# A strided and local attention with a gated MLP on one core: another kernel's planner numbers for batches 0 to 2, the planner's engine rule fixed later on, one ring for each x tile, new keys for batches 3 to 7

## The chip, the cores and the metric

One NeuronCore of a Trainium2 chip runs the kernel. The time is the device time of one launch in microseconds (us). Of the kernel before there are three timed runs; one more execution was profiled, and every time of a single instruction is from that one. PE is TensorE (matmul), PEld its weight loads, DVE VectorE, ACT ScalarE, POOL GpSimd, SP SyncE, which issues all DMAs of this kernel.

## The reference, cut to what matters

```python
# q, k, v: (8, 8, 576, 64): batch, heads, sequence, head size; everything in fp32
scores = q @ k.T / 8
mask_local   = (rel >= 0) & (rel < 32)                  # heads 0 to 3, rel = row - column
mask_strided = (rel >= 0) & (column % 32 == row % 32)   # heads 4 to 7
attn = softmax(where(mask, scores, -1e9))
x = heads side by side of (attn @ v)                    # (8, 576, 512)
h = relu(x @ w_in)                                      # w_in: 512 x 1024
u, v = h[..., :512], h[..., 512:]
v_n = (v - mean(v)) / sqrt(var(v) + 1e-6)               # over the last axis
v_s = einsum('ts,bsd->btd', w_spatial, v_n) + b_spatial[None, :, None]   # 576 x 576
out = (u * v_s) @ w_out                                 # w_out: 512 x 512
```

## The kernel before, in words

**Work.** The kernel goes through eight batches. A batch has four **x tiles** (t = 4 x batch + hp), each of 128 rows (two heads) by 576 columns; hp 0 and 1 are pairs of local heads (`local_attention`), hp 2 and 3 of strided heads (`strided_attention`). For each: scores on PE (L565 local, L711 strided), the softmax on DVE and ACT (in the first batches with a mask that DVE applies while it takes the maximum, L602), a transpose on DVE (L646, L765), copies into a sparse block layout (`ptl`, `pts`; ACT or POOL), the product with v (L675 and L781, called the PV product), and the copy of the result into x (`evac_x`).

fp32 operands of large products are held as two numbers, a high part (`rnd`, L427 on ACT, L429 on DVE or POOL) and a low part (`rest`, L437, a subtraction with two SBUF operands or one in PSUM); a product takes three matmuls (high x high, high x low, low x high). So every weight and every activation is split before PE can use it. The weights come in as 64-bit words and are first turned into fp32 by a few steps on ACT, POOL and DVE (L866, L875, L883), w_out is also combined into seven blocks (L902), and `spatial_weights` splits the spatial weights into `wsp_sb`.

Per batch follow: **V** (`v_tile`, L1034: four blocks of 128 rows, one of the 64 rows left over, the "tail", which from batch 2 on is made for two batches at once); the chain of the normalisation (`chain`: relu on ACT L992, statistics on DVE L997 and L1001 and L1005, a power on POOL L1010, the scaling on DVE L1017), a split of the result into `vn`; **U** (L1234 in batches 0 to 2; in batches 3 to 7 a Strassen form, `moe_u`, L1157); the **spatial** product (L1331, the tail's part L1343 and L1344), the gate (L1354, L1356); the **output product** in a Strassen form (L1435, its additions L1463) and the store (L1456).

**What sets the order.** All instructions go through `Program.add(key, choices, fn, reads, writes, ...)`. `Program.order()` then walks over a model of the engines: whenever an engine is free it takes the ready operation with the lowest key, and for an operation with several choices it picks the engine on which it would end first by the model's costs. The order so found is written out as it is; each engine runs its instructions in that order, and waits for what they need. DMAs (`load`) are in that order too, all on SyncE. The keys come from the table `KEYS`: "a" for the attention tiles of batches 0 and 1, "lq" and "lw" for their loads, "v", "u", "s", "t", "o" for the weights and "lv", "lu", "ls", "lo" for their loads, "fill" and "set" for clearing buffers, "p", "b" and "p2", "b2" for the steps of the output product, "cl", "ta", "la", "su", "tu" for the later batches. "dp" is a handicap that DVE gets in the choice between DVE and POOL (one number for operations with two SBUF operands that lock the port, one for the others), until "dpt" (in thousands of ns of the model's time); `SLOWED` is the model's slowdown when DVE and POOL work side by side. "w" sets where PE gets idle matmuls on zeros (L1622) to hold its clock.

**Buffers.** `r_x` holds two rings of four x tiles, one for batch 1 and its like, one for the others. The second is also the place into which the spatial weights are loaded before they are split (`spatial_weights`), and later a place for weights (`raw_slots`). `kbd` holds the strided keys, two halves that are filled and read in turn; `xt` (`r_xt`) holds the values of a strided tile or the tail rows, and `w_out_sb`, while no weights are in it, the q and v of the first strided tiles (`early_q`, `early_v`).

## Time and profile before

| | |
|---|---|
| median of 3 runs | 517.21 us (516.7 to 517.56) |
| profiled execution | 518.85 us |
| its span, from first to last instruction | 517.0 us |
| PE busy | 494.2 us (96%) |
| DVE busy | 407.8 us (79%) |
| ACT busy | 270.9 us (52%) |
| POOL busy | 142.3 us (28%) |
| mean granted clock of PE | 0.979 |
| DMA | 52.65 MB, 102 GB/s over the span |

The profiled execution is 1.85 us longer than its span (what lies around the instructions) and 1.64 us above the median of the timed runs. A line of a timeline is start, duration, engine, line, operation, output <- inputs, shape, how many were merged, and in brackets how long the engine waited for what. A line of a group has the number of instructions, their busy time, the mean of one in ns and the idle time ahead of them. In a chain or a timeline "PE L1331" is line 1331 of the kernel.

### The profile page before, as it was taken

Reading aid. Unit: us, or ns where it says so; the run is one execution under the profiler, and the core shown is the slowest. Engines: PE = TensorE matmul, PEld = TensorE weight load, DVE = VectorE, ACT = ScalarE, POOL = GpSimd, SP = SyncE. Lnnn points to the kernel's source line nnn. Section 1 sums busy time; section 2 is a strip of 40 time slices with the busy share of each in tenths; the row PEclk is TensorE's granted clock in tenths of the full one; section 3 lists DMA queues with packets and bytes.
Section 4 is the critical chain, followed back from the end, with each engine's and each line's share of the span. In section 5 each row is a group of like instructions: output and inputs, shape, how many; then the busy total and the mean of one; then the engine's idle time right before and its main releaser. Section 6 shows DMA issues by size and latency. Waiting matters only on the chain.

```text
span 517.0 us, 14639 instructions
## 1 busy us (share of the span) xinstructions
PE 494.2 (96%) x5824; PEld 451.1 (87%) x5824; DVE 407.8 (79%) x1140; ACT 270.9 (52%) x801; POOL 142.3 (28%) x256
## 2 busy tenths in 40 slices
PE   6779979999999999899999999999999998999997
PEld 4558879989899899899899998999899997899897
DVE  2799899969489769998699958997699648784566
ACT  5786765569453685476354646457264414241222
POOL 3455864043222134211131306212120102210200
PEclk9688989999999999999999999999999999999999
DMA  8796522444035413233033603324030300011002
GB/s 273 296 335 231 182 83 81 168 123 135 2 125 159 144 49 115 93 112 109 2 119 113 195 2 94 115 67 129 1 97 20 115 1 2 1 46 47 1 1 93
DMA packets 26244, 52.65 MB, mean 102 GB/s; under 512 B 3136, under 2 KB 11584, under 8 KB 26176
## 3 DMA queue, kind: packets, MB, share of 16 engines
q1 hardware_dynamic: 26176, 51.72, 30.1%
q8 instruction: 46, 0.75, 0.6%
q14 instruction: 22, 0.18, 0.1%
HBM read 42.27 MB, written 9.44 MB: 100 GB/s over the span
## 4 chain that ended last, share of the span: by engine, by line
PE 79%; DVE 10%; DMA 4%; POOL 2%; ACT 2%; issue 1%; SPq 1%; POOLq 0%; DVEq 0%; ACTq 0%
PE m L1034 17%; PE m L1331 17%; PE m L1435 15%; PE m L1157 10%; PE m L1234 5%; PE po L781 4%; PE po L675 3%; PE s L565 2%; PE m L1343 2%; DMA outT<-vv 2%; PE s L711 1%; DVE x L437 1%; DVE vn L437 1%; PE m L1344 1%; DMA k<-kT 1%
## 5 line engine op out<-in xcount | busy, mean ns | idle before, releaser
L1331 PE MATMUL m<-wsp_sb,vn 128*128 128x288 f32 x720 | 106.4, 299 | 5.3 <-DVE wsp_sb L437 3.8
L1331 PEld LDWEIGHTS m<-wsp_sb,vn 128*128 128x128 f32 x720 | 100.1, 191 | 7.4 <-DVE wsp_sb L437 4.1
L1034 PE MATMUL m<-w_in_sb,x 128*128 128x512 f32 (+1 forms) x408 | 100.9, 403 | 0.0
L1034 PEld LDWEIGHTS m<-w_in_sb,x 128*128 128x128 f32 (+1 forms) x408 | 75.5, 188 | 19.4 <-DVE x L437 0.2
L992 ACT ACTIVATE vv<-m 128x512 f32<-128x512 f32 (+1 forms) x37 | 21.8, 596 | 65.8 <-PE m L1034 65.3
L429 POOL TENSOR_SCALAR ptl<-pc 32x320 f32<-32x320 f32 (+3 forms) x86 | 41.5, 483 | 53.1 <-PE po L675 18.8
L1435 PE MATMUL m<-g,w_out_sb 128*128 128x288 f32 x384 | 55.5, 296 | 0.0
L622 ACT ACTIVATE pl<-pl,ml 128x64 f32<-128x64 f32 (+1 forms) x140 | 47.2, 341 | 15.3 <-DVE ml L602 15.1
L1010 POOL TENSOR_TENSOR bn<-bn,sel 128x1 f32<-128x1 f32 (+1 forms) x37 | 21.8, 593 | 115.1 <-DVE bn L1005 114.1
L1435 PEld LDWEIGHTS m<-g,w_out_sb 128*128 128x128 f32 x384 | 52.4, 188 | 0.3 <-DVE o L1463 0.2
L1435 PE MATMUL m<-vn,w_out_sb 128*128 128x288 f32 x288 | 42.1, 297 | 0.0
L997 DVE BATCH_NORM_STATS2 bn<-vv 128x6 f32<-128x512 f32 (+1 forms) x37 | 25.4, 686 | 19.8 <-ACT vv L992 19.5
L429 POOL TENSOR_SCALAR pts<-pc 32x288 f32<-32x288 f32 x37 | 17.5, 472 | 84.8 <-DVE pc L765 59.1
L1234 PE MATMUL m<-x,w_in_sb 128*128 128x288 f32 x288 | 40.2, 297 | 0.0
L1435 PEld LDWEIGHTS m<-vn,w_out_sb 128*128 128x128 f32 x288 | 39.2, 188 | 0.7 <-DVE o L1463 0.2
L427 ACT COPY ptl<-pc 32x64 f32<-32x64 f32 (+3 forms) x106 | 36.4, 345 | 6.0 <-DVE pc L646 3.1
L1234 PEld LDWEIGHTS m<-x,w_in_sb 128*128 128x128 f32 x288 | 38.8, 188 | 0.7
L1017 DVE TENSOR_SCALAR vv<-vv,bn 128x512 f32<-128x512 f32 (+1 forms) x37 | 21.2, 572 | 13.9 <-POOL bn L1010 13.7
L427 ACT CAST g<-u 128x576 fp32r<-128x576 f32 (+1 forms) x33 | 20.0, 610 | 19.2 <-DVE u L1356 12.7
L1168 DVE TENSOR_TENSOR u<-m,vv 128x288 f32<-128x288 f32 x30 | 13.4, 449 | 18.7 <-PE m L1157 18.6
L622 ACT ACTIVATION_READ_ACCUMULATOR pl<-pl,ml 128x1 f32 (+1 forms) x140 | 26.8, 191 | 0.0
L437 DVE TENSOR_TENSOR g<-u,g 128x576 fp32r<-128x576 f32 (+1 forms) x40 | 24.5, 631 | 0.8 <-ACT g L427 0.7
(187 smaller groups left out, 967.1 us busy)
## 6 DMA issues: line engine op xcount, KB each, us to landing
q<-qT SPq DMA_DIRECT2D x30, 295.0 KB, 4.2
outT<-o SPq DMA_DIRECT2D x48, 144.0 KB, 1.8
k<-kT SPq DMA_DIRECT2D x16, 304.0 KB, 4.3
kbd<-ks SPq DMA_DIRECT2D x32, 144.0 KB, 3.6
v_raw<-vl SPq DMA_DIRECT2D x11, 384.0 KB, 5.0
v_raw<-vs SPq DMA_DIRECT2D x8, 512.0 KB, 5.1
xt<-vs SPq DMA_DIRECT2D x7, 512.0 KB, 3.6
outT<-vv SPq DMA_DIRECT2D x16, 144.0 KB, 1.8
```

What stands on the lines that cost most here:

```text
L427: eng.copy(dst(), src())
L429: eng.tensor_scalar(dst(), src(), 1.0, 0.0, op0=ALU.mult, op1=ALU.add)
L437: eng.tensor_tensor(dst(), src(), f32(hi()), op=ALU.subtract)
L622: eng.activation(p_sb()[:m, u, :], src, AF.Exp, bias=st()[:m, u : u + 1], scale=SCALE if masked else -1.0, **total,)
L992: lambda eng: eng.activation(v()[:m], v_ps()[:m, :], AF.Relu), [(v_ps,)], [(v,)],
L997: lambda eng: eng.bn_stats(bn()[:m, 0:6], v()[:m]), [(v,)], [(bn,)],
L1010: lambda eng: eng.tensor_tensor(bn()[:m, 9:10], bn()[:m, 8:9], sel[:m, 0:1], op=ALU.pow),
L1034: eng.matmul(v_ps()[:m, :], x_at(kt)[:, a, :], w_in_sb[:, w, kt, HF:], start=(n == 0 and i == 0), stop=(n == NT - 1 and i == 2),)
L1157: eng.matmul(o_ps()[:, :HS], w_at(w)[:, a * P : (a + 1) * P], x_at(j), start=first and kk == 0 and i == 0, stop=kk == 1 and i == 2, skip_g ...
L1234: eng.matmul(u_ps()[:, :HS], w_in_sb[:, w, kt, f * P : (f + 1) * P], xs[NHP * b + kt]()[:, a, r], start=(n == 0 and i == 0), stop=(n == NT ...
L1331: eng.matmul(s_ps()[:, :HS], vn()[:, a, kt, fs], wsp_sb[:, w, kt, r], start=(kt == 0 and i == 0), stop=False,)
L1435: eng.matmul(o_ps()[:, :HS], w_out_sb()[:, b_at, w, kk, a * P : (a + 1) * P], at(j, kk), start=first and kk == 0 and i == 0, stop=kk == 1 ...
```

## The change

The functions `next_x`, `pv` and `weight` are new, and so is the field `turn` of a buffer.

* **Planner's numbers.** All keys of `KEYS` are replaced. Those that bear on batches 0 to 2 are another kernel's, those for batches 3 to 7 are new. So are the model's costs of POOL: 125 for 200 in `rnd`, 170 for 245 in its blocked form, 150 for 190 in `lowest`, the slowdowns in `SLOWED`, and a weight of 2 for POOL there (`weight`). The normalisation's scaling is counted as a light user of the port (`share=2`).
* **Engine rule.** The handicap "dp" now holds only to 125 us of the model's time; from there on it is `HELD`, the pair of numbers that was in force before all along.
* **Rings.** `r_x` is now eight rings of one tile. `next_x` gives them out: 0, 1, 2, 3 to 7 for batches 0 and 1 and the spatial weights in the order in which they ask, then 0, 1, 2; later tiles take 3 + t mod 4. Since a ring of one has no order among its tiles, `turn` makes a tile wait for the first use of the one handed out before it, in the early batches. `raw_slots` takes rings 7, 0, 1, 2.
* **PV key.** From batch 3 on the PV product's key is moved by "pv" (9.73 later-batch local tiles, 0.08 strided, -202.13 from tile 28 on; it is subtracted).

```diff
-    "a": (-7906.0, -7964.0, -15830.5, -4267.6, 1379.5, 702.2, 2039.1, -3334.8,),
+    "a": (-8700.2, -14417.0, -7800.0, -6389.1, 679.9, 5260.8, 7132.0, -3152.0,),
...
-    "dp": (12894.8, -1038.4,),
-    "dpt": (657.16,),
+    "dp": (6774.7, -492.7,),
+    "dpt": (125.0,),
...
+    "pv": (9.73, 0.08, -202.13,),
...
+HELD = (12894.8, -1038.4)
...
-SLOWED = ((0.3, 0.15), (0.45, 0.6), (0.9, 0.8))
+SLOWED = ((0.2, 0.3), (0.33, 1.2), (1.2, 0.5))
...
-                if buf.n >= buf.ring.bufs:
+                if buf.n > buf.ring.bufs:
                     deps.update(buf.last.users[:1])
+                if buf.turn is not None:
+                    deps.update(buf.turn.users[:1])
...
+        def weight(n, e):
+            return 2 if e == POOL and self.share[n] else self.share[n]
...
-                    slow = SLOWED[max(share, self.share[n])]
+                    slow = SLOWED[max(share, weight(n, e))]
...
-            held = KEYS["dp"][locks] if now < KEYS["dpt"][0] * 1000.0 else 0.0
+            held = (KEYS["dp"] if now < KEYS["dpt"][0] * 1000.0 else HELD)[locks]
...
-    r_x = [Ring(sb, f"x{i}", [P, 2, S], F32R, NHP) for i in range(2)]
+    r_x = [Ring(sb, f"x{i}", [P, 2, S], F32R, 1) for i in range(2 * NHP)]
+    x_made, x_next = [], iter([0, 1, 2, *range(3, 8), 0, 1, 2])
...
-        cost = {ACT: 110 + 0.87 * n, DVE: 70 + 0.52 * n, POOL: 200 + (1.65 if apart else 1.0) * n}
+        cost = {ACT: 110 + 0.87 * n, DVE: 70 + 0.52 * n, POOL: 125 + (1.65 if apart else 1.0) * n}
...
-        x_homes = [r_x[1].new() for _ in range(NHP)]
+        x_homes = [r_x[i].new() for i in (7, 0, 1, 2)]
...
-                due - 1.5, [(PE, 6 * 98)], f_v, [*vin, *ptok], [(o_ps,)],
+                due - 1.5 - pv(t), [(PE, 6 * 98)], f_v, [*vin, *ptok], [(o_ps,)],
...
+    def next_x(t=None):
+        at = next(x_next) if t is None or t < LEAD * NHP else 3 + t % NHP
+        buf = r_x[at].new()
+        if len(x_made) > 8 and (t is None or t < ALONE):
+            buf.turn = x_made[-1]
+        x_made.append(buf)
+        return buf
+
+    def pv(t):
+        return KEYS["pv"][2 if t >= 28 else t % NHP // 2] if t >= ALONE else 0.0
...
-        xs[t] = r_x[b == 1].new()
+        xs[t] = next_x(t)
...
-                buf = r_x[1].new()
+                buf = next_x()
```

In the changed kernel the lines behind the table are shifted: L565 is L573, L602 is L610, L437 is L445, L457 is L465, L1034 is L1057 and L1331 is L1354. The order has 1434 rows on PE (1419 before), 1125 on DVE (1131), 523 on ACT (512), 219 on POOL (207) and 182 on SyncE (184).

On SyncE, the first loads of the program; `w_out_sb <- qT` and `kbd <- ks` are the q and k of a strided tile, `q_0` and `k_0` those of a local tile, `xt <- vs` and `v_raw` are values, `vn <- w_in` is a weight. Before:

```order
L457 DMA w_out_sb_84<-qT 128x590
L457 DMA xt_87<-vs 128x1024
L457 DMA cst_sb<-cst 128x192
L457 DMA o_98<-eye 128x128
L457 DMA vn_101<-w_in 128x1024
L457 DMA kbd<-ks 64x576 x2
L457 DMA q_0_123<-qT 128x590
L457 DMA k_0_134<-kT 128x608
L457 DMA v_raw_0_140<-vl 128x768
```

and now:

```order
L465 DMA cst_sb<-cst 128x192
L465 DMA vn_85<-w_in 128x1024
L465 DMA o_92<-eye 128x128
L465 DMA q_0_94<-qT 128x590
L465 DMA k_0_100<-kT 128x608
L465 DMA q_0_107<-qT 128x590
L465 DMA k_0_121<-kT 128x608
L465 DMA v_raw_0_135<-vl 128x768
L465 DMA xt_177<-vs 128x1024
```

The q and k of a local tile moved ahead of everything of the strided ones, and both local tiles come first.

Also on SyncE, the later loads of batch 0, where the `kbd` rows for the second strided tile's successor wait until the scores before them have read the buffer. Before:

```order
L457 DMA w_out_sb_84<-qT 128x590
L457 DMA kbd<-ks 64x576 x2
L457 DMA w_out_sb_84<-vs 128x1024
L457 DMA q_1_336<-qT 128x590
L457 DMA g_378<-w_in 128x1024
L457 DMA kbd<-ks 64x576 x2
L457 DMA vn_101<-w_in 128x1024
L457 DMA g_377<-w_in 128x1024
```

and now:

```order
L465 DMA w_out_sb_228<-qT 128x590
L465 DMA kbd<-ks 64x576 x2
L465 DMA w_out_sb_228<-vs 128x1024
L465 DMA g_347<-w_in 128x1024
L465 DMA q_1_390<-qT 128x590
L465 DMA kbd<-ks 64x576 x2
L465 DMA u_291<-w_in 128x1024
L465 DMA q_1_432<-qT 128x590
L465 DMA v_raw_1_477<-vs 128x1024
L465 DMA kbd<-ks 64x576 x2
```

Behind the `kbd` rows that overwrite the buffer there stand loads of w_in, before and now, and now one more pair of q and v loads.

On DVE, the end of the stretch between the last x tile of batch 0 and the first spatial product; `pl_75 <- s` (with a second instruction that writes `ml_77`) is a masked maximum of a local tile of batch 1, `vv` and `vn` belong to the normalisation of batch 0, `g` to w_out, `wsp_sb` to the spatial weights. Before, with rows between them that are alike:

```order
L437 TENSOR_TENSOR vn_767<-vv_841,vn_767 128x512
L437 TENSOR_TENSOR w_out_sb_822<-g_648,w_out_sb_822 128x256
L602 ISA pl_75,ml_77<-s_777,cst_sb 128x64
L602 ISA ml_77 128x1
L602 ISA pl_75,ml_77<-s_779,cst_sb 128x64
L602 ISA ml_77 128x1
...
L437 TENSOR_TENSOR w_out_sb_822<-g_735,w_out_sb_822 128x256 x2
L437 TENSOR_TENSOR wsp_sb<-x_0_604,wsp_sb 128x576 x2
```

and now:

```order
L445 TENSOR_TENSOR w_out_sb_895<-g_638,w_out_sb_895 128x256 x2
L445 TENSOR_TENSOR vn_742<-vv_837,vn_742 128x512
L445 TENSOR_TENSOR wsp_sb<-x_0_714,wsp_sb 128x576
L1005 TENSOR_TENSOR wt_b<-x_0_843,wt_b 96x576
L610 ISA pl_76,ml_78<-s_744,cst_sb 128x64
L610 ISA ml_78 128x1
```

The maxima of the next local tile, which stood ahead of the last split of the spatial weights, now stand behind it, and so does a part of w_out.

64 lines of the change are left out of this document (34 added, 30 removed), and 8 rows, old and new, of the table KEYS.

## The prediction

> **What bounds the kernel now.** First the busy times of the page, then the same by stage (the stretches are mine: two halves of the head, then the batches), then the chain of waits, then the timelines of PE and DVE in the head. The page:
>
> ```profile
> PE 494.2 (96%) x5824; PEld 451.1 (87%) x5824; DVE 407.8 (79%) x1140; ACT 270.9 (52%) x801; POOL 142.3 (28%) x256
> ```
>
> By stretch (length, then PE, PEld, DVE, ACT, POOL busy, granted clock, share of the DMA engines, GB/s):
>
> ```profile
> 0.00:35.00 35.00, 24.82 (x472) 16.33 (x472) 21.25 (x48) 24.31 (x63) 15.69 (x35) 0.85 0.84 292
> 35.00:70.00 35.00, 30.84 (x351) 26.93 (x352) 32.28 (x97) 25.77 (x83) 24.52 (x30) 0.89 0.64 222
> 70.00:205.00 135.00, 135.00 (x1864) 123.90 (x1864) 110.27 (x369) 82.95 (x287) 42.83 (x84) 0.99 0.32 103
> 205.00:335.00 130.00, 127.86 (x1586) 118.86 (x1586) 111.39 (x312) 69.10 (x203) 33.16 (x62) 1.00 0.30 98
> 335.00:517.00 182.00, 175.72 (x1557) 165.04 (x1555) 132.59 (x318) 68.74 (x169) 26.07 (x48) 1.00 0.14 44
> ```
>
> PE is the bound, and from 70 to 205 us it has no gap at all. A new order can only win where PE waits: 10.2 us and 4.2 us in the two parts of the head (with a low clock there), 2.1 us in 205 to 335, 6.3 us in the rest, the last store among them. So the head decides. The chain of waits shows what holds PE there (start, duration):
>
> ```profile
> 61.32 1.26 DVE vn L437
> 66.79 1.35 DVE wsp_sb L437 x2
> 68.18 8.00 PE m L1331 x47
> 79.31 1.60 PE m L1331 x12
> ```
>
> and PE's own timeline in the head:
>
> ```profile
> 8.91 0.76 PE L711 MATMUL m<-kbd,w_out_sb 128*32 128x36 f32 x64 [1.09 <-DMA kbd<-ks]
> 11.12 1.34 PE L565 MATMUL m<-k,q 64*32 64x64 f32 x72 [1.45 <-DMA k<-kT]
> 43.20 3.06 PE L1034 MATMUL m<-w_in_sb,x 128*128 128x512 f32 x12
> 61.33 2.92 PE L1034 MATMUL m<-w_in_sb,x 128*64 128x512 f32 x12
> 68.18 4.15 PE L1331 MATMUL m<-wsp_sb,vn 128*128 128x288 f32 x18 [3.79 <-DVE wsp_sb L437]
> ```
>
> PE ends the work it has at 64.25 (61.33 + 2.92), waits 3.79 us for DVE's last split of the spatial weights, and then runs the first 48 spatial matmuls in 8.00 us where 12 of them later take 1.60, so 48 would take 6.4. Half the clock costs 1.6 us more. Behind that, PE never waits until 205. So the time at which the first spatial product starts (68.18) moves the end of the kernel one for one, as long as nothing behind it becomes late.
>
> What sets 68.18 is DVE: from the last x tile of batch 0 on it works without a break to the last split. The x tiles of batch 0 (their low halves, the last step of each):
>
> ```profile
> 21.76 0.96 DVE L437 TENSOR_TENSOR x<-po,x 128x288 fp32r<-128x288 f32 x2
> 27.92 0.78 DVE L437 TENSOR_TENSOR x<-po,x 128x288 fp32r<-128x288 f32 x2
> 38.09 0.81 DVE L437 TENSOR_TENSOR x<-po,x 128x288 fp32r<-128x288 f32 x2
> ```
>
> The first is done at 22.7, the first local one at 28.7, the last at 38.9; the split ends at 68.1 (66.79 + 1.35). These are two pieces: 38.9 us to the last x tile, and some 29.2 us of DVE work.
>
> **Term 1, the first tiles.** The loads before the first scores change, as the order of SyncE shows: before, q and k of the first local tile are behind seven others, now behind three (cst, w_in, eye). Their sizes, from the DMA issues (the fourth column is KB):
>
> ```profile
> q<-qT SPq DMA_DIRECT2D x30, 295.0 KB, 4.2
> k<-kT SPq DMA_DIRECT2D x16, 304.0 KB, 4.3
> kbd<-ks SPq DMA_DIRECT2D x32, 144.0 KB, 3.6
> xt<-vs SPq DMA_DIRECT2D x7, 512.0 KB, 3.6
> vn<-w_in SPq DMA_DIRECT2D x4, 512.0 KB, 5.7
> ```
>
> With cst (128x192 in fp32, 96 KB) and eye (64 KB): before 295 + 512 + 96 + 64 + 512 + 2 x 144 + 295 + 304 = 2366 KB, now 96 + 512 + 64 + 295 + 304 = 1271 KB. 1095 KB less is 1.12 MB, and at the 292 GB/s of the first stretch that is 3.8 us: local scores at 7.3, not 11.12. From first scores to a finished x tile the strided tile took 13.8 us (8.91 to 22.7) and the local one 17.6 (11.12 to 28.7), the latter with the strided tile in front of it on DVE and ACT. So the first x tile now comes between 21.1 and 24.9. I take 21.6, near the low end, since the local tile now has DVE to itself; that is 1.1 before the 22.7.
>
> From the first to the last x tile before took 16.2 us (22.7 to 38.9). At that pace the last one now comes at 37.8. DVE's order has about 1.1 us less other work in between (36.7), and if only the landings of the loads counted it would be 35. I take the middle, 35.9: **3.0 us earlier**. Bounds: 1.1 later (a first x tile at 24.9 with the 1.1 us less) and 3.9 earlier.
>
> **Term 2, the DVE stretch behind it.** In DVE's order 84 rows stand between the last x tile and the last split before, 62 now. The rows of that stretch by shape (busy, mean ns of one):
>
> ```profile
> L437 DVE TENSOR_TENSOR vn<-vv,vn 128x512 fp32r<-128x512 f32 x4 | 3.7, 951 | 0.0
> L437 DVE TENSOR_TENSOR w_out_sb<-g,w_out_sb 128x256 fp32r<-128x256 f32 x4 | 2.5, 642 | 0.0
> L437 DVE TENSOR_TENSOR wsp_sb<-x,wsp_sb 128x576 fp32r<-128x576 f32 x3 | 2.1, 741 | 0.0
> L437 DVE TENSOR_TENSOR w_in_sb<-vn,w_in_sb 128x512 fp32r<-128x512 f32 x1 | 1.1, 1128 | 0.0
> L437 DVE TENSOR_TENSOR w_in_sb<-g,w_in_sb 128x512 fp32r<-128x512 f32 x1 | 1.1, 1103 | 0.0
> L437 DVE TENSOR_TENSOR w_in_sb<-u,w_in_sb 128x512 fp32r<-128x512 f32 x1 | 0.6, 629 | 0.0
> L883 DVE SCALAR_TENSOR_TENSOR u<-u 128x512 int32<-128x512 int32 x1 | 0.7, 677 | 0.0
> L902 DVE TENSOR_TENSOR g<-g 128x256 f32<-128x256 f32 x1 | 0.4, 422 | 0.0
> L602 DVE CUSTOM_DVE_ANT_0 pl<-s,cst_sb 128x64 f32<-128x64 f32 x16 | 2.7, 210 | 1.2 <-PE s L565 1.2
> ```
>
> Out of the stretch go 10 masked maxima of the next local tile (2.7 / 16 = 0.17 each, 1.7), 2 low halves of w_out (0.64 each, 1.3), 1 of the spatial weights (0.74), 1 of w_in (0.95, the mean of 1.13, 1.10 and 0.63) and 1 word step of L883 (0.68); 2 combinations of w_out come in (0.42 each, 0.84). Sum: 1.7 + 1.3 + 0.74 + 0.95 + 0.68 - 0.84 = **4.5 us less**. Bounds: 2.6, if what leaves are the cheap ones, and 7.4, if the rows that stay also lose the time they now lose beside POOL (rival a).
>
> Spatial start by both terms: 68.2 - 3.0 - 4.5 = 60.7. PE itself is there 21.05 us after the first product with the last x tile (43.20 to 64.25), and the order has 222 rows ahead of the first spatial product in both kernels, so at 35.9 + 21.05 = 57.0 at the earliest. PE still waits 3.7 us for DVE, so DVE's time counts in full, and the slow clock behind the wait stays as it is.
>
> The Trainium skill, "TensorE: Matmul & The Clock Gate" (What's actually happening), says that PE falls to half rate after an idle window of about 3.4 us; the 3.79 us of waiting and the 8.00 us behind it agree. By that rule the half rate would vanish were the wait under 3.4 us, and the sum would be 1.6 us lower; by my 3.7 us it stays.
>
> **Term 3, the work that was moved.** The 4.5 us are not gone: the maxima, splits and steps now stand behind the first spatial product. DVE has little room there:
>
> ```profile
> 80.00:90.00 10.00, 10.00 (x155) 9.74 (x156) 9.67 (x27) 4.74 (x14) 4.11 (x4) 1.00 0.16 52
> 90.00:100.00 10.00, 10.00 (x80) 9.63 (x77) 9.99 (x46) 6.27 (x28) 0.84 (x2) 1.00 0.48 156
> 100.00:110.00 10.00, 10.00 (x175) 7.92 (x175) 6.81 (x32) 6.36 (x28) 3.53 (x8) 1.00 0.31 97
> ```
>
> It is full from 80 to 100 and has 3.2 us free from 100 to 110. So 4.5 - 3.2 = **1.3 us** can come back as a wait of PE for the operands of batch 0's output product or of batch 1's V. Bounds 0 and 4.5.
>
> **Term 4, batches 3 to 7.** The new keys there, the early or late PV product and the x rings of one tile move rows on every engine, but PE waits only 2.1 us between 205 and 335 and 6.3 us after that. Typical of these waits is one for the tail rows:
>
> ```profile
> 210.54 0.98 DVE tail L437
> ```
>
> I take nothing for it: some tails get less PE work in front of them and some less DVE work. Bounds: 1.5 us either way, the price of one or two such waits more or fewer. The rings cost no instruction; SBUF holds the same eight tiles. The rule for choosing between DVE and POOL adds none either, it only places them.
>
> **Sum.** -3.0 - 4.5 + 1.3 + 0 = -6.2 us. Against the profiled execution (518.85 us, a span of 517.0): 512.7, span 510.8. It lies 1.6 us above the median of the three runs; against that median, 517.2 - 6.2 = **511.0 us**. Two runs of this kernel differ by up to 0.86 us, so about 0.2% (1 us) can be told from no change.
>
> **Rival a, PE binds.** The low halves of DVE take 951 ns (vn) and 1128 ns (w_in) on average in the stretch, while alone they take
>
> ```profile
> 51.48 0.68 DVE L437 TENSOR_TENSOR vn<-vv,vn 128x512 fp32r<-128x512 f32 x1
> ```
>
> 0.68 (vn) and 0.63 (w_in, in the third of the rows above). Were the new order to let them run alone, it would save 4 x 0.27 + 2 x 0.48, and on w_out 4 x 0.22 (0.642 against the 0.422 of L902 on the same shape), 2.9 us more: DVE would be at 57.8, and with 0.9 more of the lead at PE's own 57.0. Then the start moves by 11.2, the wait and the half clock go (1.6), and 1.3 come back: 517.2 - 11.5 = 505.7. For it: the new keys are made with other costs of this contention. Against it: POOL's order has as many two-input operations beside the stretch as before. Chance 0.18.
>
> **Rival b, given back to POOL.** In POOL's order four low halves of w_out now stand nearly in a row in the stretch. On POOL they take (with the longest one)
>
> ```profile
> L437 POOL TENSOR_TENSOR w_out_sb<-g,w_out_sb 128x256 fp32r<-128x256 f32 x3 | 3.4, 1137 | 0.1
> L437 POOL TENSOR_TENSOR wsp_sb<-x,wsp_sb 128x576 fp32r<-128x576 f32 x1 | 1.4, 1407 | 0.1
> ```
>
> If each held up DVE's low half beside it for all of its 1.137 us, that would be 4.5 us, as much as the stretch saves. Only the lead of 3.0 would stay: 514.2, and with the moved work returning as well up to 516. For it: vn's 951 against 0.68. Against it: before has such pairs too, and lost 0.27 of them on average, not 1.1. Chance 0.20. The Trainium skill, "SBUF — State Buffer" (Who interferes with whom), says that the port pair which DVE and GpSimd share is an exclusive lock, so that a DVE operation with two SBUF inputs is fully blocked beside a GpSimd one that reads SBUF. By that rule this rival, not the forecast, is the likelier; the trace's 951 against 0.68 lies nearer to a part of a block than to a whole one.
>
> **Rival c, slower: SyncE stands.** Before, SyncE waited ahead of
>
> ```profile
> 22.51 1.12 SPq L457 DMA_DIRECT2D kbd<-ks  x2
> ```
>
> until the strided scores had read the buffer. Now the same kind of load (the second pair of kbd rows in SyncE's order) stands behind scores that come after the PV product of the first local tile, and ahead of a load of w_in that the first V product needs. I expect it at about 22 again. Every microsecond beyond some 24 delays the loads behind it, the x tiles and the first spatial product alike. At 30 all of the 6.2 us are lost, beyond that the kernel is slower: at 33, 520 us. For it: the local tile goes first, so strided scores come later. Against it: the first scores are 3.8 us earlier. Chance 0.17.
>
> **How the numbers follow.** The forecast has 0.45. Of rival b about two thirds are faster by over 0.2% (0.13), the rest within it; rival c is slower but for 0.02. Faster 0.45 + 0.18 + 0.13 = 0.76, same 0.07 + 0.02 = 0.09, slower 0.15. The forecast's own range is 507.6 to 514.4: half of the spans of terms 1 (5.0) and 3 (4.5), taken as independent, make 3.4 either way. The range for 8 in 10 goes from rival a less the 1.5 us of term 4 (504) to just above no change (517.5): rival c's rest (0.15) and some 0.04 below 504 are left out.
>
> **What would show it.** In the changed kernel's profile: local scores near 7.3, a first x tile near 21.6, the last of batch 0 near 36, the first spatial product near 61 after a wait of 3 to 4 us, then half the clock for some 8 us; PE with at most 1 or 2 us of waits between 61 and 205; waits behind 205 like before. Wrong in one step: no wait ahead of the spatial product (rival a), a last x tile near 36 but the product after 64 (rival b), a SyncE load of kbd issued after 24 (rival c). Wrong as a whole: a stretch between 70 and 205, or behind 335, in which PE loses more than 2 us.

## The result, and the profile after

The changed kernel takes 520.15 us (median of 11 runs, 518.59 to 522.92), the kernel before 517.24 us on the same chip (11 runs, 515.31 to 518.39). The ratio is 1.0066, with a 95% interval of 1.0045 to 1.0087: slower by 2.9 us, where 6.2 us less were forecast and 517.5 was the upper end of the range.

One trace is one execution, and this difference is as small as that between two executions of one kernel. So a second trace of each was taken. The four executions are 518.59 and 521.97 us for the changed kernel (span 516.8 and 520.2; the first is the fastest of its 11 runs) and 518.85 and 516.97 us for the one before (517.0 and 515.1). The mean of the changed kernel's two, 520.3, is close to its median; that of the other two, 517.9, is 0.7 above its own. Lines are below mostly from the second executions, and sums are made from all four.

The page's busy times of the changed kernel (first execution) barely differ from those before; PE has the same work, and it still binds:

```profile
PE 493.6 (96%) x5820; PEld 450.1 (87%) x5820; DVE 409.0 (79%) x1131; ACT 271.0 (52%) x797; POOL 152.1 (29%) x269
```

By stretch (length, then PE, PEld, DVE, ACT, POOL, granted clock, DMA share, GB/s), the changed kernel's second execution:

```profile
0.00:35.00 35.00, 25.92 (x568) 17.60 (x569) 22.68 (x54) 24.56 (x65) 18.68 (x37) 0.90 0.90 315
35.00:70.00 35.00, 30.75 (x274) 27.28 (x273) 31.58 (x95) 27.36 (x83) 23.20 (x29) 0.95 0.59 202
70.00:205.00 135.00, 134.79 (x1916) 123.33 (x1918) 112.49 (x368) 85.35 (x288) 48.30 (x96) 1.00 0.34 106
205.00:335.00 130.00, 126.71 (x1538) 117.73 (x1524) 108.37 (x303) 66.59 (x199) 34.23 (x59) 0.99 0.29 94
335.00:520.00 185.00, 177.68 (x1552) 166.02 (x1550) 133.65 (x315) 66.88 (x166) 28.24 (x50) 0.99 0.13 43
```

and the second one before:

```profile
205.00:335.00 130.00, 127.64 (x1585) 118.66 (x1584) 111.17 (x311) 69.28 (x203) 32.81 (x60) 1.00 0.29 94
335.00:515.00 180.00, 174.13 (x1546) 163.58 (x1544) 131.14 (x315) 68.30 (x168) 26.09 (x48) 1.00 0.13 45
```

Up to 35 us the granted clock is 0.85 in the first execution of either kernel and 0.90 in the second, so there it tells executions apart and not kernels; from 35 to 70 us it is 0.95 in both executions of the changed kernel against 0.89 and 0.92. Behind 205 us PE idles 3.3 us of 130 where it idled 2.4, and behind 335 us 7.3 where it idled 5.9 (second executions). A matmul at half clock counts as busy for longer (twelve take 3.16 us instead of 1.86, below), so busy time hides part of the loss. PE's timeline of the changed kernel's second execution shows the places:

```profile
7.76 0.97 PE L573 MATMUL m<-k,q 64*32 64x64 f32 x72
15.04 1.19 PE L719 MATMUL m<-kbd,w_out_sb 128*32 128x36 f32 x64 [4.83 <-DMA kbd<-ks]
64.91 7.05 PE L1354 MATMUL m<-wsp_sb,vn 128*128 128x288 f32 x41 [3.06 <-DVE wsp_sb L445]
209.37 0.40 PE L1366 MATMUL m<-wt_h,tail 128*128 128x288 f32 x1 [1.78 <-DVE tail L445]
211.24 3.16 PE L1354 MATMUL m<-wsp_sb,vn 128*128 128x288 f32 x12
328.48 0.40 PE L1366 MATMUL m<-wt_h,tail 128*128 128x288 f32 x1 [1.17 <-DVE tail L445]
444.96 0.40 PE L1366 MATMUL m<-wt_h,tail 128*128 128x288 f32 x1 [1.27 <-DVE tail L445]
446.46 2.93 PE L1354 MATMUL m<-wsp_sb,vn 128*128 128x288 f32 x12 [0.17 <-DVE u L1379]
```

and the same places in the second execution before:

```profile
65.58 4.69 PE L1331 MATMUL m<-wsp_sb,vn 128*128 128x288 f32 x18 [3.50 <-DVE wsp_sb L437]
208.87 0.40 PE L1343 MATMUL m<-wt_h,tail 128*128 128x288 f32 x1 [0.42 <-DVE tail L437]
211.58 1.86 PE L1331 MATMUL m<-wsp_sb,vn 128*128 128x288 f32 x12 [1.37 <-DVE u L1354]
328.28 0.40 PE L1343 MATMUL m<-wt_h,tail 128*128 128x288 f32 x1
442.24 0.40 PE L1343 MATMUL m<-wt_h,tail 128*128 128x288 f32 x1 [0.77 <-DVE tail L437]
```

The first spatial product starts 0.7 us earlier (64.91 against 65.58; 64.10 against 68.18 in the first executions). Then the three tail waits of batches 2, 4 and 6, which were 0.42, 0 and 0.77 us, are 1.78, 1.17 and 1.27 us, and behind those of batches 2 and 6 twelve spatial matmuls take 3.16 and 2.93 us instead of 1.86. The granted clock (the number before the DMA share) shows why they do in that execution:

```profile
208.00:210.00 2.00, 0.63 (x4) 0.64 (x5) 1.65 (x3) 1.21 (x2) 1.68 (x2) 1.00 0.93 318
210.00:212.00 2.00, 1.87 (x12) 1.63 (x11) 1.97 (x6) 0.42 (x1) 0.00 (x0) 0.84 0.35 130
212.00:214.00 2.00, 2.00 (x10) 2.00 (x10) 2.00 (x5) 1.35 (x3) 0.00 (x0) 0.50 0.00 0
446.00:448.00 2.00, 1.83 (x11) 1.60 (x10) 1.99 (x5) 1.14 (x2) 0.00 (x0) 0.72 0.00 0
```

Its first execution has the same tail waits and no such fall (the first row is the first spatial product):

```profile
64.10 7.21 PE L1354 MATMUL m<-wsp_sb,vn 128*128 128x288 f32 x41 [2.20 <-DVE wsp_sb L445]
208.89 0.41 PE L1366 MATMUL m<-wt_h,tail 128*128 128x288 f32 x1 [1.77 <-DVE tail L445]
210.76 1.86 PE L1354 MATMUL m<-wsp_sb,vn 128*128 128x288 f32 x12
444.36 1.86 PE L1354 MATMUL m<-wsp_sb,vn 128*128 128x288 f32 x12 [0.16 <-DVE u L1379]
```

To add this up, here is an account of what PE loses: the start of a matmul less the time that all matmuls ahead of it take at undisturbed pace (0.133 us for one of 128x288, from 12 in 1.60; 0.233 for one of 128x512, from 48 in 11.20; the same for the scores and PV products). The whole work is 461.2 us in both kernels by this pace, so whatever an account shows on top is time lost, whatever the order; its absolute level hangs on the pace taken for the smallest matmuls, the differences between kernels to 0.4 us. Microseconds lost up to a time, in each of the four executions (the last columns: up to the last matmul, and from its start to the end of the span):

```
up to           80    200   215   320   340   420   447   460   last  behind
before, 1st    33.5  38.9  41.4  45.0  45.8  48.3  51.5  51.5  52.2   3.67
before, 2nd    31.8  37.5  39.7  43.5  44.3  46.4  49.6  49.6  50.3   3.67
changed, 1st   29.0  35.1  37.7  41.0  43.1  45.9  50.2  50.4  51.2   4.36
changed, 2nd   29.6  35.6  39.7  43.0  45.1  48.0  52.4  53.8  54.9   4.09
mean changed
less before    -3.4  -2.9  -1.9  -2.3  -1.0  -0.4  +0.8  +1.6  +1.9   +0.6
```

The change does win in the head: 3.4 us at 80 us. It gives back 0.5 by 200, then 1.0 at the tail rows of batch 2 (200 to 215), 1.3 at those of batch 4 (320 to 340), 0.6 from there to 420, 2.3 from 420, just ahead of the tail rows of batch 6, to the last matmul, and 0.6 behind it, with 0.4 won in between (215 to 320). The mean span is 2.45 us longer (518.5 against 516.05).

Read by execution, the account splits the loss behind 200 us. At batch 2 (200 to 215) the first execution of the changed kernel loses 2.6 us where the kernel before loses 2.5 and 2.2: the longer tail wait (1.77) stands in for a tail wait of 0.42 and a wait of 1.4 for the gate behind it. Only the second one, with the fall of the clock, loses 4.1. At batch 4 (320 to 340) both executions lose 2.1 where both before lose 0.8, and from 420 to 447 they lose 4.3 and 4.4 where both before lose 3.2, at full clock up to 446 us. From 200 us to the end of the span the changed kernel loses 3.8 us more than the mean of before in its first execution and 6.7 in its second.

### The profile page after: what moved, and what is told of

It reads as the page before. It is cut to its first block, busy times and chain, and to the rows that moved or that the text cites. A ratio compares the mean times of both kernels' runs of the same rounds, so it can differ in the third digit from the quotient of the medians.

```text
span 516.8 us, 14629 instructions
## 1 busy us (share of the span) xinstructions
PE 493.6 (96%) x5820; PEld 450.1 (87%) x5820; DVE 409.0 (79%) x1131; ACT 271.0 (52%) x797; POOL 152.1 (29%) x269
## 4 chain that ended last, share of the span: by engine, by line
PE 72%; DVE 16%; DMA 5%; ACT 2%; POOL 2%; issue 1%; SPq 1%; POOLq 0%; DVEq 0%; ACTq 0%
PE m L1057 16%; PE m L1458 15%; PE m L1354 15%; PE m L1180 10%; PE m L1257 4%; PE po L683 2%; PE po L789 2%; DVE vn L445 2%; DVE x L445 2%; PE s L573 2%; DVE x L925 2%; PE s L719 1%; DMA x<-wsp 1%; PE m L1366 1%; PE m L1367 1%
## 5 line engine op out<-in xcount | busy, mean ns | idle before, releaser
L1354 PE MATMUL m<-wsp_sb,vn 128*128 128x288 f32 x720 | 109.4, 299 | 2.8 <-DVE wsp_sb L445 2.2
L1354 PEld LDWEIGHTS m<-wsp_sb,vn 128*128 128x128 f32 x720 | 101.2, 192 | 5.3 <-DVE wsp_sb L445 2.4
L1057 PE MATMUL m<-w_in_sb,x 128*128 128x512 f32 (+1 forms) x408 | 98.6, 397 | 1.6 <-DVE w_in_sb L445 1.3
L1057 PEld LDWEIGHTS m<-w_in_sb,x 128*128 128x128 f32 (+1 forms) x408 | 74.5, 185 | 20.7 <-DVE w_in_sb L445 1.6
L437 POOL TENSOR_SCALAR ptl<-pc 32x64 f32<-32x64 f32 (+3 forms) x95 | 41.8, 440 | 61.1 <-DVE pc L654 25.0
L1458 PE MATMUL m<-g,w_out_sb 128*128 128x288 f32 x384 | 58.4, 297 | 0.0
L1033 POOL TENSOR_TENSOR bn<-bn,sel 128x1 f32<-128x1 f32 (+1 forms) x37 | 23.0, 625 | 118.8 <-DVE bn L1028 113.2
L435 ACT COPY ptl<-pc 32x320 f32<-32x320 f32 (+3 forms) x97 | 34.4, 355 | 5.8 <-DVE pc L654 2.4
L437 POOL TENSOR_SCALAR pts<-pc 32x288 f32<-32x288 f32 x36 | 17.9, 498 | 64.8 <-DVE pc L773 38.9
L457 ACT COPY vv<-m 128x288 f32<-128x288 f32 x26 | 10.3, 398 | 33.4 <-PE m L1458 28.3
```

The lines of the kernel that those rows point to most:

```text
L435: eng.copy(dst(), src())
L437: eng.tensor_scalar(dst(), src(), 1.0, 0.0, op0=ALU.mult, op1=ALU.add)
L1033: lambda eng: eng.tensor_tensor(bn()[:m, 9:10], bn()[:m, 8:9], sel[:m, 0:1], op=ALU.pow),
L1057: eng.matmul(v_ps()[:m, :], x_at(kt)[:, a, :], w_in_sb[:, w, kt, HF:], start=(n == 0 and i == 0), stop=(n == NT - 1 and i == 2),)
L1354: eng.matmul(s_ps()[:, :HS], vn()[:, a, kt, fs], wsp_sb[:, w, kt, r], start=(kt == 0 and i == 0), stop=False,)
L1458: eng.matmul(o_ps()[:, :HS], w_out_sb()[:, b_at, w, kk, a * P : (a + 1) * P], at(j, kk), start=first and kk == 0 and i == 0, stop=kk == 1 ...
```

## The experiments

Three causes stood against each other: that the new order makes the tail rows late, and the clock falls behind these waits; that the loss lies in the head, which won less than forecast; or that one part alone (late keys, early keys, rings, durations, engine rule) brings it. Medians are in microseconds, ratios against the kernel before on the same chip.

**Second executions.** Both kernels unchanged.

> The changed kernel once more, for a second trace: the first trace is of its fastest execution (518.6 of 518.6 to 522.9 us), so it cannot show where the median loses. Theory A (late keys: the waits for tail rows and operands behind 205 us give back what the head wins): the same head as the first trace, first spatial product at 64, and some 2 to 4 us more of waits of PE behind 205. Theory B (the head itself is unsteady): a first spatial product later than 65 in this trace, the rest as in the first. Time 520 by either.

> The kernel before once more, for a second trace: its first trace is of an execution of 518.85 us, above all its timed runs. Theory A (the changed kernel wins in the head and loses behind it): the first spatial product again at 67 to 69, so that the head of the changed kernel (64.1 and 64.9) is 3 to 5 us ahead. Theory B (most of the head's gain is only that the first trace of before was a poor one): first spatial product at 65 to 66.5.

The changed kernel took 520.33 (518.75 to 521.97), ratio 1.0060 with 1.0037 to 1.0083; one more execution of the kernel before took 516.97. The slowdown repeats. The tail waits stand in both traced executions of the changed kernel (1.77, 1.18 and 1.28 us in the first), the falls of the clock in the slower one. The kernel before started its first spatial product at 65.58 us in this execution, as theory B has it, so a good part of the 4.1 us by which the first traces differ there is that between two executions of one kernel. By the account the changed kernel is still 2.2 to 2.8 us ahead of this execution at 80 us, and behind it at the end.

**The later keys of before in the changed kernel** (batches 3 to 7: the groups below, the other groups as changed):

```diff
-    "p2": (24.22, 30.06, 1.53,),
+    "p2": (11.39, 28.77, 1.25,),
...
-    "pv": (9.73, 0.08, -202.13,),
+    "pv": (0.0, 0.0, 0.0,),
...
-    "su": (-9.09, 297.28,),
+    "su": (240.79, 97.41,),
```

> The changed kernel with the keys for the later batches (p2, b2, cl, ta, la, su, tu; pv at zero) of before. Theory A: the head's 4 us stay and the later batches lose what they lost before: 514 to 516, faster than before by over 0.2%. Theory B (the loss is in the head or in batches 0 to 2): 519 to 521, as the changed kernel.

533.67 (531.91 to 537.39), ratio 1.0327 (1.0292 to 1.0361).

**The early keys of before in the changed kernel** (all other groups, and with `dp` and `dpt` the engine rule of before):

```diff
-    "a": (-8700.2, -14417.0, -7800.0, -6389.1, 679.9, 5260.8, 7132.0, -3152.0,),
+    "a": (-7906.0, -7964.0, -15830.5, -4267.6, 1379.5, 702.2, 2039.1, -3334.8,),
...
-    "dp": (6774.7, -492.7,),
+    "dp": (12894.8, -1038.4,),
```

> The changed kernel with all other keys of before, that is the order of batches 0 to 2 and the engine rule of before, with the new keys for the later batches. Theory A: it has no gain in the head and all of the loss behind it, 521 to 524. Theory B: no loss, 516 to 518.

529.62 (528.88 to 530.60), ratio 1.0237 (1.0210 to 1.0265).

**Only the rings, in the kernel before** (its keys and durations on eight rings of one tile):

```diff
-    r_x = [Ring(sb, f"x{i}", [P, 2, S], F32R, NHP) for i in range(2)]
+    r_x = [Ring(sb, f"x{i}", [P, 2, S], F32R, 1) for i in range(2 * NHP)]
+    x_made, x_next = [], iter([0, 1, 2, *range(3, 8), 0, 1, 2])
...
```

> Before with the eight rings of one tile alone: all keys and costs of before. Theories A and B: no difference beyond 1 us, 516.5 to 518.5. Theory C (the rings and their turns order the tiles so that loads or splits come later): slower by 2 to 3 us, 519 to 520.

534.88 (533.09 to 536.33), ratio 1.0333 (1.0304 to 1.0361). The rings issue nothing, and yet in the kernel before they cost 17 us: the planner sees other dependences and writes another order.

**Only the rings undone, in the changed kernel** (two rings of four):

```diff
-    r_x = [Ring(sb, f"x{i}", [P, 2, S], F32R, 1) for i in range(2 * NHP)]
+    r_x = [Ring(sb, f"x{i}", [P, 2, S], F32R, NHP) for i in range(2)]
...
```

> The changed kernel with the two rings of four x tiles of before, and all else as changed. Theory A (the new keys are made for the eight rings; either structure is as good with keys of its own): 525 to 535, much slower, as the rings alone under the old keys were (534.9). Rival (the rings themselves cost time, in any order): 515 to 518, faster than the changed kernel.

545.08 (544.05 to 548.00), ratio 1.0545 (1.0517 to 1.0574).

**Only the early or late PV product undone:**

```diff
-    "pv": (9.73, 0.08, -202.13,),
+    "pv": (0.0, 0.0, 0.0,),
```

> The changed kernel with the new key for the PV product at zero, so that it stands where before had it; all other keys new. Theory A (each of the new keys is only good beside the others, as the four undone parts at 530 to 545 say): 522 to 528. Rival (the moved PV products are what makes the tails late behind 205 us): 517 to 519.

527.68 (526.51 to 529.24), ratio 1.0204 (1.0170 to 1.0237).

**Only the fixed engine rule undone** (the rule of the early batches goes on to the end):

```diff
-HELD = (12894.8, -1038.4)
+HELD = (6774.7, -492.7)
```

> The changed kernel with the early handicap of DVE against POOL (6774.7, -492.7) in force all along, instead of the pair of before from 125 us of the model's time on. The orders are the same up to some 165 us; behind that 11 rows fewer stand on DVE and 17 more on POOL. Theory A (DVE is full at 195 to 216 and 320 to 332, and that makes PE's waits there): these waits shrink by what DVE is rid of, 518 to 519.5. Rival (each part is only good beside the others, since the order behind any change is another one): 523 to 530.

538.29 (536.32 to 541.30), ratio 1.0415 (1.0372 to 1.0459).

**Only the planner's durations undone:**

```diff
-SLOWED = ((0.2, 0.3), (0.33, 1.2), (1.2, 0.5))
+SLOWED = ((0.3, 0.15), (0.45, 0.6), (0.9, 0.8))
...
-            return 2 if e == POOL and self.share[n] else self.share[n]
+            return self.share[n]
...
-        cost = {ACT: 110 + 0.87 * n, DVE: 70 + 0.52 * n, POOL: 125 + (1.65 if apart else 1.0) * n}
+        cost = {ACT: 110 + 0.87 * n, DVE: 70 + 0.52 * n, POOL: 200 + (1.65 if apart else 1.0) * n}
```

> The changed kernel with the planner's costs of before (POOL's three constants, the slowdowns, the weight and the share of the scaling), all keys and rings new. By the rival above 523 to 535; if the costs do not matter, 519 to 521.

525.65 (524.72 to 527.30), ratio 1.0167 (1.0133 to 1.0201).

Seven mixtures of the two kernels lie between 525.7 and 545.1, all slower than either, and five of them slower than every range written for them (only the PV key and the durations came out within one). So undoing no part wins the 2.9 us back. That doesn't clear the parts: each mixture is planned into another order, in which the rest may fit worse, and the price of a part in the whole kernel isn't among these numbers. What the change costs has to be read from places in the whole kernel.

**The tail waits, taken away by their data.** The tail matmuls of batches 2, 4 and 6 read weights that have been there since the start, in place of the tail rows, so what they compute is left out; the order is the same on every engine. In the changed kernel and, line for line, in the one before:

```diff
-                    eng.matmul(o, tl()[:, fs], wt_h[:, r], start=False, stop=False)
-                    eng.matmul(o, tb[:97, fs], wt_b[:97, r], start=False, stop=True)
+                    eng.matmul(o, (wt_h if b in (2, 4, 6) else tl())[:, fs], wt_h[:, r], start=False, stop=False)
+                    eng.matmul(o, (wt_b if b in (2, 4, 6) else tb)[:97, fs], wt_b[:97, r], start=False, stop=True)
```

> The changed kernel in its own order, but in batches 2, 4 and 6 the tail's two matmuls read the weight tile as their stationary operand and not the tail rows, so that PE no longer waits for those (the output of these batches is not the reference's). Theory A (the loss is the wait for tail rows, 4.2 us in both traces, and the low clock behind it in the second one): 514 to 515.5 us, and runs closer together. Theory B (the wait only moves to the next operand, the gate or the output product): 518 to 520.

> The same edit on the kernel before, in its own order (again the output of batches 2, 4 and 6 is not the reference's). Its trace has 1.2 us of such waits. Theory A: 515.5 to 516.5, so that without these waits the changed kernel is the faster of the two by 1 us or more. Theory B: no change, 517.

Changed: 522.16 (520.10 to 525.24), ratio 1.0094 (1.0060 to 1.0129). Before: 518.23 (516.17 to 519.68), 1.0006 (0.9988 to 1.0024). Nothing is won in either, and the changed one came out above both of its ranges. The list of PE's waits in the changed kernel's run names no tail any more, but the gates behind it (sum, count, longest):

```profile
PE m L1354 <- DVE u L1379: 3.4, 2, 1.7
PE m L1354 <- DVE u L1377: 2.2, 1, 2.2
```

PE passes the tails without a wait and then stands for the gate product `u`, which DVE makes right behind them. So the tail is only the first of DVE's products to show that DVE is late there, and the first cause doesn't hold in its simple form.

**The tails' chain pulled forward.** The operations that make paired tails go ahead in the order of ACT, POOL and DVE as soon as their inputs are there; PE's order stays. In both kernels:

```diff
+        ends = {}
+        for i, (at, n, e) in enumerate(issued):
+            if n in self.soon:
+                at = min(at, max(ends[d] for d in self.ops[n][3]) + 200.0)
+                issued[i] = (at, n, e)
+            ends[n] = at + dict(self.ops[n][1])[e]
+        issued = sorted(issued, key=lambda x: x[0])
```

> The changed kernel with the steps of the paired tails (statistics, power, scaling, split) pulled forward to where their inputs are ready, in the orders of ACT, POOL and DVE; PE's order is the same. Theory A (the order makes the tails late): the waits ahead of the tail's matmuls at 209 and 326 us, 1.8 and 1.2 us, are gone, and with the one at 211 the low clock behind it: 517 to 518.5. Rival (DVE is full there, and the wait moves to the gates or to the next product): 519.5 to 521.

> The same edit on the kernel before, whose waits there are 1.2 us for the tail and 1.4 us for a gate. Theory A: 515.5 to 516.5. Rival: 517 to 518.

Changed: 520.58 (517.97 to 521.85), ratio 1.0061 (1.0036 to 1.0086), the same as without the edit. Before: 518.48 (517.50 to 520.16), 1.0023 (1.0008 to 1.0039), a little slower. In the changed kernel batch 2's tail is split by 207.8 us instead of 210.3, but its gate `u` comes no sooner (210.91 against 210.73): PE waits for it, now 2.10 us, and the stretches ahead of it show DVE full (third busy time):

```profile
211.41 3.15 PE L1364 MATMUL m<-wsp_sb,vn 128*128 128x288 f32 x12 [2.10 <-DVE u L1387]
```

```profile
195.00:200.00 5.00, 5.00 (x31) 4.52 (x30) 4.96 (x10) 3.46 (x7) 2.51 (x5) 1.00 0.26 80
200.00:205.00 5.00, 5.00 (x61) 4.72 (x63) 4.93 (x9) 2.76 (x6) 4.61 (x5) 1.00 0.02 6
205.00:210.00 5.00, 4.31 (x114) 3.95 (x113) 4.84 (x7) 0.40 (x1) 1.02 (x2) 1.00 0.75 244
```

At batch 2, pulling one DVE chain ahead pushes another back. DVE is as full around batch 4's tail (11.77 and 11.80 us busy of the 12 from 320 us on). At batch 6 it isn't (9.81 and 10.55 of the 12 from 436 us on), so what holds the tail there isn't shown.

**Matmuls on zeros ahead of the tails**, so that PE isn't idle in the wait. In batches 2, 4 and 6, into the unused part of the group:

```diff
+                    if f == 0 and hf == 0 and b in (2, 4, 6):
+                        for _ in range(3):
+                            eng.matmul(
+                                s_ps()[:STRIDE, :WARM_COLS], zeros,
+                                zeros[:, None, :].to_broadcast([P, WARM_COLS // STRIDE, STRIDE]),
+                                start=False, stop=False,
+                            )
```

> The changed kernel with three matmuls on zeros (adding zero to an accumulator that PE has at hand, some 1.4 us) ahead of the tail's first matmul in batches 2, 4 and 6, where PE waits for 1.2 to 1.8 us anyway. Theory A (in the median execution the clock falls to half behind these waits, as in the second trace at 211 and 446): 518 to 519, and the runs within 2.5 us. Theory B (the low clock there comes with the run, not with the waits, or is rare): 520 to 520.5.

519.29 (516.73 to 522.44, 12 runs), ratio 1.0041 (1.0016 to 1.0066). In the trace the clock doesn't fall behind the tails (1.00 granted from 206 to 216 and from 442 to 452 us), and what is left of the tail waits is 1.1 us:

```profile
PE m L1373 <- DVE tail L445: 1.1, 2, 0.7
```

The median is 0.9 us under the changed kernel's 520.15, with intervals that overlap, so the falls of the clock are worth about a third of the 2.9 us by the medians, and this isn't settled. The runs still spread over 5.7 us, where under 2.5 was expected, so if the zeros keep the clock up in every run, the falls aren't what spreads them. The rest of the slowdown is there without a fall, as in the first execution of the changed kernel.

**Zeros ahead of the first spatial product, too.** In the kernel before, six calls in its 3.5 to 3.8 us wait; in the changed kernel four there and the three at the tails:

```diff
+                            if (b, hf, f, kt, i) == (0, 0, 0, 0, 1):
+                                for _ in range(6):
+                                    eng.matmul(
+                                        s_ps()[:STRIDE, :WARM_COLS], zeros,
...
```

> The kernel before with six matmuls on zeros (2.7 us, adding zero to an accumulator) in the wait of PE for DVE ahead of the first spatial product, which is 3.5 to 4.3 us long in its three traces. Theory A (the half clock behind that wait costs 1.6 us, as 48 matmuls in 8.00 us for 6.4 say): 515 to 516, faster than before by 1.2 to 2.2 us. Rival (PE is then early and waits for the tail rows of batch 0 instead, as the changed kernel did with the w_out steps moved): 517, no change.

> The changed kernel with the fillers at the tails (as before, 519.3 us) and four more (1.8 us) in its wait ahead of the first spatial product, which is 2.2 to 3.8 us long. Theory A (the clock): 517 to 518, and still 2 us behind before with the same fillers, which is then the waits' part. Rival (the tail rows of batch 0 take over): 519 to 520.

Before: 517.71 (516.15 to 520.51, 12 runs), ratio 1.0016 (0.9995 to 1.0037). Changed: 521.06 (520.36 to 522.78), 1.0076 (1.0051 to 1.0101). In the kernel before the half clock is gone, 47 matmuls in 6.45 us where it was 8.00 and 8.90 in the two executions without zeros, and the next product of twelve waits for a gate:

```profile
67.24 6.45 PE L1338 MATMUL m<-wsp_sb,vn 128*128 128x288 f32 x47 [1.26 <-DVE wsp_sb L437]
77.46 1.86 PE L1338 MATMUL m<-wsp_sb,vn 128*128 128x288 f32 x12 [0.64 <-DVE u L1361]
```

Its account stands at 31.9 us at 80 and 51.6 at the last matmul; without zeros it was 33.5 and 31.8 at 80, 52.2 and 50.3 at the last. The 1.6 us that the half clock cost by the forecast are not there at the end: the interval leaves room for a gain of 0.05% (0.3 us) at most.

In the changed kernel with both sets of zeros the tail waits shrink to 0.4 us and no fall of the clock stands at the tails, but PE now waits 3.0 us for ACT's copies out of `m` (`vv`, L457), where it waited 0.4 and 0.5 us in the two executions without zeros:

```profile
PE m L1180 <- ACT vv L457: 3.0, 3, 1.5
```

So in that trace a lead of PE ends behind ACT too, and not behind DVE alone.

**The second w_out tile later.** Its three word steps (on ACT, POOL and DVE) and what depends on them go behind the last split of the spatial weights, since DVE waited for them in the stretch:

```diff
+        late, at = {355, 356, 357}, [n for _, n, _ in issued].index(20)
+        for _, n, _ in issued[: at + 1]:
+            if self.ops[n][3] & late:
+                late.add(n)
+        head = issued[: at + 1]
+        issued = [x for x in head if x[1] not in late] + [x for x in head if x[1] in late] + issued[at + 1 :]
```

> The changed kernel with one piece of its order moved: the word steps of the second w_out tile (on ACT, POOL and DVE) and what needs them go behind the last split of the spatial weights, so that nothing of batch 0's normalisation stands behind the load of w_out that lands at 53.5 us; all else in place. Theory A (that load, through the queues of POOL and DVE, holds DVE up for 1 to 2.5 us ahead of the first spatial product): the last split done by 60 to 62, PE waits under 1 us, no low clock behind it, 3 to 5 us less lost by 72; at the end 516 to 518. Rival (DVE is full from 75 to 100, so that the moved work makes PE wait there): the first product just as early, but the gain gone by 105, 519.5 to 521.

527.67 (523.74 to 531.01), ratio 1.0192 (1.0145 to 1.0238). PE's timeline:

```profile
63.99 4.48 PE L1360 MATMUL m<-wsp_sb,vn 128*128 128x288 f32 x32 [0.40 <-DVE wsp_sb L451]
78.36 0.61 PE L1372 MATMUL m<-wt_h,tail 128*128 128x288 f32 x1 [7.06 <-DVE tail L451]
```

The wait ahead of the spatial product went from 3.06 to 0.40, and one of 7.06 for the first tail took its place. The loads of the next two w_out tiles go out at 70.18 us, behind the moved steps, and in the changed kernel itself at 63.31: what was taken out of the stretch comes back right behind it, with interest.

**Both edits**, the w_out steps later and the zeros at the tails:

```diff
+        late, at = {355, 356, 357}, [n for _, n, _ in issued].index(20)
...
+                    if f == 0 and hf == 0 and b in (2, 4, 6):
...
```

> Both edits together. Theory A in both cases: 514 to 516, faster than before. If only the first holds 516 to 518, if only the second 518 to 519, if neither 520 to 521.

523.77 (523.05 to 524.58), ratio 1.0128 (1.0098 to 1.0157). None of the versions beats the kernel before.

## Why the prediction was wrong, step by step

The forecast was -6.2 us; the mean of the traces is +2.45 (the timed medians +2.9). By the account the miss of 8.65 us is made of 4.15 us less won in the head (-3.35 measured by 80 us, -7.5 expected from terms 1 and 2), 0.8 us less given back in term 3, and 5.3 us lost behind 200 us (0.6 of them behind the last matmul), where term 4 had nothing. So terms 1 and 2 were sized too large, and term 4 was missing. The range of 3.4 us either way was also too narrow by its own rows: it takes in the spans of terms 1 and 3 and leaves out those of term 2 (2.6 to 7.4) and term 4 (1.5 either way).

**The step that failed** is term 4: "I take nothing for it: some tails get less PE work in front of them and some less DVE work. Bounds: 1.5 us either way". From 200 us on the changed kernel loses 5.3 us more than the one before: 3.8 in the execution without a fall of the clock and 6.7 in the other. I had sized the term by one or two single waits, without asking which engine is late there. The head's lead reaches the tails on PE, and DVE doesn't hand it on. DVE's timeline around batch 2's tail, changed kernel and before (second executions):

```profile
199.06 0.68 DVE L1020 BATCH_NORM_STATS2 bn<-vv 128x6 f32<-128x512 f32 x1
205.29 0.17 DVE L1024 BATCH_NORM_AGGREGATE bn<-bn 128x2 f32<-128x6 f32 x1
207.40 0.55 DVE L1040 TENSOR_SCALAR vv<-vv,bn 128x512 f32<-128x512 f32 x1 [0.45 <-POOL bn L1033]
208.63 1.71 DVE L445 TENSOR_TENSOR tail<-vv,tail 64x512 fp32r<-64x512 f32 x2 [0.32 <-ACT tail L435]
```

```profile
203.17 0.68 DVE L997 BATCH_NORM_STATS2 bn<-vv 128x6 f32<-128x512 f32 x1
204.43 0.17 DVE L1001 BATCH_NORM_AGGREGATE bn<-bn 128x2 f32<-128x6 f32 x1
206.59 0.54 DVE L1017 TENSOR_SCALAR vv<-vv,bn 128x512 f32<-128x512 f32 x1
207.83 2.01 DVE L437 TENSOR_TENSOR tail<-vv,tail 64x512 fp32r<-64x512 f32 x2
```

The tail's statistics come 4.1 us earlier than before (199.06 against 203.17), but the next step of its chain, the aggregation, only at 205.29: between the two DVE has 5.5 us of other combinations and splits in its order (L925, L445), where it had 0.6 before. So the normalised rows come at 207.40, 0.8 us later than before; in the first executions they come 1.4 us earlier (206.92 against 208.28). On the mean DVE is 0.3 us ahead there, and PE was 2.9 ahead at 200 us. So PE waits. At batch 2 that alone costs no more than the two waits before did; the tail of batch 4 then waits 1.2 us where none was, that of batch 6 1.3 where 0.8 was, and the falls of the clock come on top in one of the two executions. Taking these waits away, by other data or by an earlier chain, wins nothing and moves them to other products of DVE, mostly the gate that it makes next, so at batches 2 and 4, where DVE is full, it is DVE's pace and not the tail alone that holds PE. Which of the new keys puts DVE's work there in that order stays open, and so do the 0.6 us between 340 and 420.

**The price of the lead was wrong in principle.** I wrote that the first spatial product's start "moves the end of the kernel one for one, as long as nothing behind it becomes late", and took the 135.00 of 135 us busy in the stretch behind it as the proof. It says that PE has work all that time; it doesn't say that DVE keeps up behind 205. The kernel before with zeros in its wait says the same: there PE alone was given time, and the end stays. A head in which DVE is ahead too does carry through: the second execution before lost 1.7 us less than the first by 80 us, had batch 2's tail rows normalised 1.7 us earlier (206.59 against 208.28), and lost 1.9 less by the last matmul.

**Term 1** had its first half right. Local scores were expected at 7.3 us and start at 8.02 and 7.76; the first x tile was expected at 21.6 and is done at 21.66 and 21.55 (20.71 + 0.84):

```profile
20.71 0.84 DVE L445 TENSOR_TENSOR x<-po,x 128x288 fp32r<-128x288 f32 x2
34.91 0.45 DVE L445 TENSOR_TENSOR x<-po,x 128x288 fp32r<-128x288 f32 x1
35.70 0.69 DVE L906 SCALAR_TENSOR_TENSOR vn<-vn 128x512 int32<-128x512 int32 x1 [0.33 <-POOL vn L898]
36.30 0.68 DVE L445 TENSOR_TENSOR w_in_sb<-vn,w_in_sb 128x512 fp32r<-128x512 f32 x1
36.91 0.45 DVE L445 TENSOR_TENSOR x<-po,x 128x288 fp32r<-128x288 f32 x1
```

The last x tile was to come at 35.9 and is done at 37.36 (36.91 + 0.45; 38.37 in the second execution before): a lead of 1.0 (1.3 in the first executions), within my bounds of 1.1 later and 3.9 earlier, but not the 3.0 that I took. The plain pace of the kernel before gave 37.8; the middle between that and two faster paces had no row behind it. Two steps for w_in stand between the two halves of that tile, and the strided scores, whose loads went behind the local ones, waited for them until 15.04 (9.02 in the second execution before).

**Term 2** was 4.5 us less in the DVE stretch from the last x tile to the last split. The whole stretch in the second executions, changed and before:

```profile
37.36:64.85 27.49, 23.30 (x236) 20.28 (x234) 24.84 (x64) 21.08 (x61) 18.89 (x23) 1.00 0.56 187
```

```profile
38.37:65.53 27.16, 22.76 (x300) 19.77 (x298) 27.16 (x87) 21.40 (x68) 22.24 (x27) 0.97 0.64 214
```

DVE has 64 instructions in place of 87 and 2.3 us less work (24.84 against 27.16; 24.18 against 26.52 in the first executions), a little under my lower bound of 2.6: what left was cheap (the maxima), the low halves of vn and w_in that stayed still last 0.98 and 1.15 us, and the two of w_out that stayed last 0.81 where they lasted 0.64. And the stretch is no shorter than in the second execution before, because DVE idles 2.65 us in it where it idled 0. The longest of these waits, and what it stands behind on POOL and SyncE:

```profile
54.26 0.69 DVE L906 SCALAR_TENSOR_TENSOR g<-g 128x512 int32<-128x512 int32 x1 [1.76 <-POOL g L898]
```

```profile
53.56 0.66 POOL L898 TENSOR_SCALAR g<-g 128x512 int32<-128x512 uint8 x1 [4.56 <-DMA g<-w_out]
```

```profile
47.73 0.33 SPq L465 DMA_DIRECT2D g<-w_out  x1
```

DVE's word step of w_out stands behind POOL's, which stands behind a load that SyncE issues at 47.73. The second execution before issued it at 43.16, but the first one at 47.77, and there DVE idled 2.7 us of 29.2 too. So the late load isn't shown to be the change's doing, and my "without a break" was wrong of the very trace that I had. I counted what leaves DVE's order, and didn't follow what the instructions that stay are fed by. On the mean of two executions each the stretch is 1.2 us shorter (27.0 against 28.2): 2.3 less work, 1.1 more idle time.

**Term 3** was about right: 0.5 us came back between 80 and 200 us, with 1.3 expected and 0 to 4.5 as bounds.

**The clock.** The half clock behind the first spatial wait is there as forecast, with a wait of 3.06 us in the second execution and 2.20 in the first: 41 matmuls take 7.05 and 7.21 us, where 5.5 would be undisturbed. The Trainium skill, "TensorE: Matmul & The Clock Gate" (What's actually happening), gives an idle window of about 3.4 us, by which neither of these waits would have halved the rate; here the measurement decides. Taking the half clock away in the kernel before won nothing at the end, so it wasn't worth its 1.6 us there.

**The rivals.** Rival c, SyncE standing, didn't happen: the kbd rows that I expected at about 22 are issued at 21.34 us (22.31 in the first execution):

```profile
21.34 1.12 SPq L465 DMA_DIRECT2D kbd<-ks  x2
```

Rival a didn't, since PE waits 3.06 us for DVE. My mark for rival c, a load of kbd after 24, was badly put, since the next pair is issued at 26.33 now and was at 27.41 before (second executions). Of rival b a little is there: the two low halves of w_out on DVE got 0.17 us dearer each (0.81 against 0.64), and those of vn and w_in no cheaper; that is far from its 4.5 us. The kernel got slower by none of the three mechanisms; the sentence that would have shown it is my last: "a stretch between 70 and 205, or behind 335, in which PE loses more than 2 us". From 340 us to the end PE and the last stores lose 3.4 us more than before.

**The end** adds 0.6 us: from the start of the last matmul to the end of the span 4.36 and 4.09 us, 3.67 in both executions before. SyncE issues the last store 0.63 and 0.35 us after DVE's last addition, where it was 0.02 before; why wasn't tried.

## What to carry to other kernels

A lead in the head is money at the end only if every engine that feeds the bound one has it too: follow it past each place where another engine is full, here DVE at the tails of batches 2 and 4, before you price it one for one. Where a planner turns keys, durations and rings into one order, undoing a part gives another order and not the part's price; read the loss from places in the whole kernel, with an account of lost time. And take several executions when the difference is one that two executions of one kernel show as well.
